# Gate and val of 256 tokens: half-block products by the seven-product scheme in place of full ones, in a dealt order, and last stores on two queues

**Chip, cores, metric.** One core of one Trainium2 chip. The metric is the device time of one execution in microseconds (us), the median over runs of one kernel on one chip.

## The reference

An attention block between 8 batches of 512 tokens and 32 state rows each (8 heads of 64) gives 8 x (512 + 32) rows of 512 values. A feed-forward block with RMS norm follows on all of them. The change concerns the feed-forward block of the 8 x 32 = 256 state rows:

```python
def _moe_ref(x, w_gate, w_val, w_out, rms_g):      # x: rows of 512, d_ff = 1536
    rms = np.sqrt(np.mean(x * x, axis=-1, keepdims=True) + 1e-06)
    xn = x / rms * rms_g
    g = xn @ w_gate
    silu = g * (1.0 / (1.0 + np.exp(-g)))
    val = xn @ w_val
    return (silu * val @ w_out).astype(np.float32)
```

## The kernel before

All is float32. The tokens of the batches come first. Gate and val of all batches but the first, and the output projections of these batches and of the states, are already done in seven products of half blocks instead of eight (the Strassen-Winograd scheme: a 2 x 2 block product costs seven half-block products, and some sums of blocks before and after). The states' 256 rows come last. Their gate and val were still full products: twelve hidden blocks m, for gate (k = 0) and val (k = 1) four contraction blocks i each, 256 columns at a time.

```python
    def hidden(m, n, lhs, rhs, banks):              # [... cut: set-up]
        def products():
            for k, to in enumerate((gp, vp)):
                to.append(banks[k].tile([P, S], F32, name=...))
                for i, r in enumerate(rhs):
                    TE.matmul(out=to[0][:, 0:n], lhsT=lhs(i, k), rhs=r,
                              start=(i == 0), stop=(i == len(rhs) - 1))
                yield
        def silu():  ...                            # ScalarE: Silu of gate, PSUM to SBUF
        def gated(): ...                            # VectorE: times val; for the upper blocks two more sums
# [... cut: the batches]
    for m in range(NM):                             # the states' stretch: NM = 12
        n = B * (NM // 2) + m // 2
        for part in hidden(m, NT, lambda i, k: w_sb[n][:, i, m % 2, k, :],
                           [xsT[:, i, :] for i in range(NI)], ((fx, fx), (fy, fz))[m % 2]):
            for _ in part:
                pass
        if m % 2:
            fetch(n + W_BUFS)                       # W_BUFS = 3: the weights of the pair after next but one
    p, c, k = project_seven(NT, store_states)       # products, copies, sums of the output projection
    for step in (p, c, p, c, k, p, k, p, c, k, p, k, p, k, p, c):
        next(step)
```

The pools of PSUM, the memory that TensorE writes its products to: a bank is one buffer of such a pool; `fx` has two banks, `fy` and `fz` one each. The weights of a pair of hidden blocks are one megabyte, in one of three buffers; a buffer is refilled when its pair has been multiplied for the last time.

## Time and profile before

| | before |
|---|---|
| time, median (runs) | 806.35 us (806.14 to 807.25, 3 runs) |
| span in the profile | 804.3 us |
| TensorE busy | 779.2 us, 97% |
| granted TensorE clock, mean | 0.989 |
| states' gate and val on TensorE | 192 records, 41.4 us |
| last copy's end to the end of the span | 3.84 us |

How to read it: the chain that ended last is the work followed back from the last instruction, at each step to what released it; the granted clock is the share of its full clock at which TensorE was let run. An engine that is busy 97% of the span and that makes up 94% of this chain is the bound; work of the others counts only where TensorE waits for it. TensorE makes two records of each float32 matmul (192 for the 96 here). The length printed for a record (379 ns) is longer than its share of the time, since records overlap; their spacing, from start to start (0.2158 us here), is what adds up. The lines are in the prediction.

### The profile page before, as it was taken

Reading aid. Unit: us, or ns where it says so; the run is one execution under the profiler, and the core shown is the slowest. Engines: PE = TensorE matmul, PEld = TensorE weight load, DVE = VectorE, ACT = ScalarE, POOL = GpSimd, SP = SyncE. Lnnn points to the kernel's source line nnn. Section 1 sums busy time; section 2 is a strip of 40 time slices with the busy share of each in tenths; the row PEclk is TensorE's granted clock in tenths of the full one; section 3 lists DMA queues with packets and bytes.
Section 4 is the critical chain, followed back from the end, with each engine's and each line's share of the span. In section 5 each row is a group of like instructions: output and inputs, shape, how many; then the busy total and the mean of one; then the engine's idle time right before and its main releaser. Section 6 shows DMA issues by size and latency. Waiting matters only on the chain.

```text
span 804.3 us, 11772 instructions
## 1 busy us (share of the span) xinstructions
PE 779.2 (97%) x4678; PEld 592.5 (74%) x4678; DVE 493.3 (61%) x746; ACT 341.1 (42%) x560; POOL 178.4 (22%) x215
## 2 busy tenths in 40 slices
PE   4599999999999999999999999999999999999997
PEld 2243444788778887888778877888788877888886
DVE  4999996588347842786368834784278626841121
ACT  4888864553245323543255324532354325401110
POOL 0000003530154005500443025400550044200000
PEclk9699999999999999999999999999999999999999
DMA  9788745600172007300460017200630035001401
GB/s 294 229 287 298 262 160 185 259 31 13 36 269 105 1 24 248 152 1 18 150 241 17 14 44 261 106 1 20 233 115 2 13 145 208 2 14 38 147 12 27
DMA packets 61591, 94.09 MB, mean 117 GB/s; under 512 B 38752, under 2 KB 46432, under 8 KB 54624
## 3 DMA queue, kind: packets, MB, share of 16 engines
q1 hardware_dynamic: 59456, 92.81, 33.4%
q8 instruction: 37, 0.61, 0.3%
q10 hardware_dynamic: 2080, 0.52, 0.3%
q14 instruction: 18, 0.15, 0.1%
HBM read 78.12 MB, written 15.20 MB: 116 GB/s over the span
## 4 chain that ended last, share of the span: by engine, by line
PE 94%; DVE 4%; issue 0%; ACT 0%; DMA 0%; SPq 0%; DVEq 0%
PE f L677 35%; PE f L527 32%; PE f L486 5%; PE f L617 5%; PE pv L486 4%; PE at L444 3%; PE pv L444 3%; PE at L273 2%; PE at L282 1%; PE at L327 1%; PE at L341 1%; PE at L388 1%; DVE ex L223 1%; PE at L376 1%; DVE raw L219 1%; PE at L252 1%
## 5 line engine op out<-in xcount | busy, mean ns | idle before, releaser
L677 PE MATMUL f<-wo,hb 128*128 128x256 f32 x540 | 124.1, 382 | 0.6 <-ACT ot L710 0.5
L527 PE MATMUL f<-aT_s,v 128*128 128x256 f32 x504 | 119.6, 381 | 0.0
L677 PEld LDWEIGHTS f<-wo,hb 128*128 128x128 f32 x540 | 101.4, 190 | 20.5 <-ACT ot L710 7.3
L527 PEld LDWEIGHTS f<-aT_s,v 128*128 128x128 f32 x504 | 93.7, 190 | 17.3 <-issue 5.2
L589 DVE TENSOR_TENSOR g<-g,f 128x512 f32<-128x512 f32 x84 | 57.6, 687 | 78.2 <-PE f L527 74.9
L245 POOL TENSOR_TENSOR ri<-ss,mhalf 128x4 f32<-128x4 f32 x8 | 9.1, 1141 | 364.4 <-DVE ss L345 364.4
L527 PE MATMUL f<-aT_t,vs 128*128 128x256 f32 x336 | 87.1, 382 | 0.0
L677 PE MATMUL f<-wt,hs 128*128 128x256 f32 x360 | 80.3, 379 | 0.0
L677 PEld LDWEIGHTS f<-wt,hs 128*128 128x128 f32 x360 | 68.4, 190 | 9.3
L527 PEld LDWEIGHTS f<-aT_t,vs 128*128 128x128 f32 x336 | 62.6, 190 | 15.4 <-issue 6.2
L710 ACT COPY ot<-f 128x256 f32<-128x256 f32 x60 | 21.4, 371 | 121.6 <-PE f L677 121.6
L580 ACT ACTIVATE hb<-g 128x1024 f32<-128x1024 f32 x42 | 44.4, 1057 | 55.0 <-DVE g L589 55.0
L591 DVE SCALAR_TENSOR_TENSOR hb<-hb,g 128x1024 f32<-128x1024 f32 x42 | 55.4, 1320 | 8.0 <-ACT hb L580 8.0
L473 POOL TENSOR_TENSOR vs<-v,vs 128x256 f32<-128x256 f32 x42 | 58.3, 1388 | 0.0
L470 POOL TENSOR_TENSOR vs<-v 128x256 f32<-128x256 f32 x42 | 30.6, 728 | 118.5 <-ACT v L455 118.5
L578 ACT COPY g<-f 128x512 f32<-128x512 f32 x42 | 24.6, 586 | 67.4 <-PE f L527 67.4
L486 PE MATMUL pv<-aT_s,v 128*128 128x512 f32 x96 | 45.2, 611 | 1.1 <-DVE aT_s L351 1.1
L617 PE MATMUL f<-wo,hb 128*128 128x512 f32 x96 | 44.7, 600 | 0.0
L527 PE MATMUL f<-aT_t,v 128*128 128x256 f32 x168 | 43.9, 383 | 0.0
L527 PE MATMUL f<-aT_s,vs 128*128 128x256 f32 x168 | 43.1, 379 | 0.0
L677 PE MATMUL f<-wt,hb 128*128 128x256 f32 x180 | 42.5, 386 | 0.0
L486 PE MATMUL f<-xsT,w_m 128*128 128x256 f32 x192 | 42.1, 379 | 0.0
(116 smaller groups left out, 1213.7 us busy)
## 6 DMA issues: line engine op xcount, KB each, us to landing
w_m<-w_d SPq DMA_DIRECT2D x48, 1024.0 KB, 6.6
x_b<-in_x_dram SPq DMA_DIRECT2D x30, 256.0 KB, 4.0
out_dram<-ot SPq DMA_DIRECT2D x56, 128.0 KB, 1.8
raw<-in_moe_w_val_dram SPq DMA_DIRECT2D x6, 1024.0 KB, 5.2
raw<-in_moe_w_out_dram SPq DMA_DIRECT2D x6, 1024.0 KB, 7.1
w_d<-w_m SPq DMA_DIRECT2D x6, 1024.0 KB, 4.9
raw<-in_moe_w_gate_dram SPq DMA_DIRECT2D x5, 1024.0 KB, 5.7
raw<-in_moe_w_gate_dram SPq DMA_DIRECT2D x2, 512.0 KB, 4.9
```

Source lines behind the costliest of these rows:

```text
L444: TE.matmul(out=pv[e][Ns * j:Ns * j + Ns, :], lhsT=stT_g[b][D * e:D * e + D, j, :], rhs=w[D * e:D * e + D, j].rearrange("p m k f -> p (m k ...
L470: GE.tensor_tensor(out=vs[:, 0], in0=a21, in1=a22, op=ALU.add)
L473: GE.tensor_tensor(out=vs[:, 2], in0=a12, in1=vs[:, 1], op=ALU.subtract)
L486: TE.matmul(out=to[0][:, 0:n], lhsT=lhs(i, k), rhs=r, start=(i == 0), stop=(i == len(rhs) - 1))
L527: TE.matmul(out=ps[:, i, :], lhsT=lhs[:, i, :], rhs=rhs, start=(start and i == 0), stop=True, skip_group_check=True)
L578: SE.copy(g[:, :, 1, :], q["x"])
L580: SE.activation(out=hb[:, 2 * mp:2 * mp + 2, :], func=ACTF.Tanh, scale=0.5, in_=g.rearrange("p m c t -> p m (c t)"))
L589: VE.tensor_tensor(out=to, in0=to, in1=q[ps], op=ALU.add)
L591: VE.scalar_tensor_tensor(out=h, in0=h, scalar=1.0, op0=ALU.add, op1=ALU.mult, in1=g.rearrange("p m c t -> p m (c t)"))
L617: TE.matmul(out=banks[r], lhsT=hb[:, m, P * r:P * r + P], rhs=wo[:, m, :], start=(m == 0), stop=(m == NM - 1))
L677: TE.matmul(out=banks[name][:, r, :], lhsT=lhs(k)[:, P * r:P * r + P], rhs=rhs(k), start=(start and r == 0 and k == 0), stop=(k == HM - 1) ...
L710: SE.copy(to, banks[name][:, r, :])
```

## The change

The intent is an eighth less work on TensorE in the states' gate and val. The function that did seven products for the batches is made general and used here too: seven products per pair of hidden blocks, each of 2 output blocks x 2 contraction blocks of 128 columns. For this VectorE must form sums of the weights (four per pair, 128x512 each) and of the tokens. Products (h), copies and Silu on ScalarE (t), sums after the products (u) and weight sums (y) are dealt to the engines by hand in one string; p, c, k are the projection. Apart from that the y-bank product of the states' projection is cut in two, and the last stores alternate between two queues.

```diff
+STATES = (
+    "hhtyythyhyyhthuhuyttuyuhhyhttuhhyhuhuhttuythyuhythuhyyhuuuhhthtythuuhtuyhhuhhtuh"
+    "yutyutuhthhhyhuuhuytuuththuhhuthuuuutuhuuppkcuppccppkkkpkpc"
+)
         # [... cut]
+    def sums_of_w(mps):
+        for mp in mps:
+            a11, a12, a21, a22 = blocks_of_w(mp)
+            ...
+            VE.tensor_tensor(out=s12[:, 0], in0=a21, in1=a22, op=ALU.add)
+            yield
+            VE.tensor_tensor(out=s12[:, 1], in0=s12[:, 0], in1=a11, op=ALU.subtract)
+            yield
+            VE.tensor_tensor(out=s4, in0=a12, in1=s12[:, 1], op=ALU.subtract)
+            yield
+            VE.tensor_tensor(out=a21, in0=a11, in1=a21, op=ALU.subtract)
+            yield
         # [... cut: views of blocks, sums of the tokens]
         def product(ps, lhs, rhs, start):
             for i in range(2):
-                TE.matmul(out=ps[:, i, :], lhsT=lhs[:, i, :], rhs=rhs, start=(start and i == 0),
-                          stop=True, skip_group_check=True)
+                for k, (l, r) in enumerate(zip(lhs, rhs)):
+                    TE.matmul(out=ps[:, i, 0:half], lhsT=l[:, i, :], rhs=r, ...)
         # [... cut: in project_seven, for the states only]
-            yield from product("y", A(0, 1), B(1, 0))
+            parts = (range(HM),) if R > 1 else (range(HM // 2), range(HM // 2, HM))
+            yield from product("y", A(0, 1), B(1, 0), parts[0])
             yield from product("x", S_, TS(1))
+            for ks in parts[1:]:
+                yield from product("y", A(0, 1), B(1, 0), ks)
         # [... cut: store_states]
-            nc.sync.dma_start(out=out[r0:r0 + Ns, c0:c0 + n], in_=...)
+            queue = (nc.sync, *more)[j % (1 + len(more))]
+            queue.dma_start(out=out[r0:r0 + Ns, c0:c0 + n], in_=...)
         # [... cut: the loop over m goes]
+    h, t, u = hidden_seven(NT, (state_weights, state_sums), state_tokens, True,
+                           lambda mp: fetch(n + mp + W_BUFS))
+    p, c, k = project_seven(NT, store_states, nc.scalar)
+    streams = {"h": h, "t": t, "u": u, "p": p, "c": c, "k": k, "y": sums_of_w(range(1, NM // 2))}
+    with tc.manual_schedule(**by_hand):
+        for stream in STATES:
+            next(streams[stream])
```

Each pair has the products x, z, x, z, y, x into the banks of these names, then the next pair's first x and z, then its own last x ("last product").

## The prediction

> **What bounds the kernel now.** I read the page's busy times first: TensorE is busy nearly the whole span and no other engine comes near it. Then the chain that ended last, from 742 us on, which is where the changed stretch lies:

> ```profile
> PE 779.2 (97%) x4678; PEld 592.5 (74%) x4678; DVE 493.3 (61%) x746; ACT 341.1 (42%) x560; POOL 178.4 (22%) x215
> ...
> 742.33 38.85 PE f L486 x180
> 781.18 10.37 PE f L677 x48
> 791.55 0.02 issue
> 791.58 0.38 ACT ot L710
> 791.96 0.04 issue
> 792.00 8.05 PE f L677 x36
> 800.05 0.02 issue
> 800.08 0.37 ACT ot L710
> ```

> L486 is gate and val of the states' 256 tokens, L677 their output projection, L710 a copy out of PSUM. The path is TensorE alone, except for 0.46 us at 791.55 (a copy stands between two products into the same bank) and the tail after 800.05. L486 runs at 38.85 / 180 = 0.2158 us per record. It has 96 matmuls of 256 columns, two records each, so 192 x 0.2158 = 41.4 us in all; 12 of the records are used earlier as filling in the last batch's projection (three gaps of 4 records, 0.86 us each). The other engines idle here: between 742.4 and 781.2 VectorE is busy 7.6 us and ScalarE 4.6 us (busy times by stretch, summed). So removing TensorE work there should shorten the kernel one for one, unless a new wait appears.

> The group rows of the old stretch, and two places elsewhere that show what a short record costs:

> ```profile
> L486 PE MATMUL f<-xsT,w_m 128*128 128x256 f32 x192 | 42.1, 379 | 0.0
> L486 PEld LDWEIGHTS f<-xsT,w_m 128*128 128x128 f32 x192 | 36.5, 190 | 5.0
> ...
> 692.67 1.84 PE L412 MATMUL at<-ones,sqT 128*128 128x1 f32 x16
> 694.38 0.89 PE L527 MATMUL f<-aT_s,v 128*128 128x256 f32 x3
> ...
> 603.13 0.60 PE L273 MATMUL at<-ident,x_b 128*128 128x128 f32 x4
> 603.57 1.03 PE L527 MATMUL f<-aT_t,v 128*128 128x256 f32 x4
> ```

> From start to start, sixteen records of one column with a full weight load each take (694.38 - 692.67) / 16 = 0.107 us: there the weight load is the bound. Four transposes of 128 columns take 0.44 / 4 = 0.11 us. The 190 ns of a load's own row is its length, not its spacing.

> [...] No float32 matmul of 128 columns that isn't a transpose is in this trace; whether two such nearly equal halves overlap fully is my largest uncertainty. [...]

> **The change part by part.**

> *Products.* Per pair of hidden blocks seven products of half blocks: 7 x 2 output blocks x 2 contraction blocks = 28 matmuls of 128 columns, 56 records; six pairs make 336 records. At 0.110 us: 37.0 us against 41.4, a gain of 4.4 us. One product (8 records) is a step of 0.88 us, there are 42 steps.

> *Added VectorE and ScalarE work.* Per pair VectorE has three sums from PSUM and two products (0.42 us each, as 128x256 sums from PSUM show), for the upper three pairs two more, and four weight sums of 128x512 (0.69 us, from such rows). In the stretch itself that is about 15 x 0.69 + 36 x 0.42 = 25.5 us of 37: no bound by quantity. ScalarE's three copies and one Silu per pair are under 2 us of each pair's 6.2.

> *Weights' arrival.* This is where I expect most of the gain to go. Only three weight buffers exist, so pairs 3, 4, 5 are fetched when pairs 0, 1, 2 have had their last product. These fetches are in the trace of before, where nothing waits for them:

> ```profile
> L143 SPq DMA_DIRECT2D w_m<-w_d x3: 320/327/327, 746.7 to 760.5; - x3
> ...
> DMA to landing us min/median/max: 4.6/4.7/4.8
> ```

> Before, such a megabyte is first read two pairs later by TensorE. Now VectorE must first make sums of it, and the dealt order of VectorE has the first sum of pair 3's weights directly behind pair 0's last product and ahead of pair 1's sum out of the z bank. Sequence after pair 0's last product ends: landing 4.75 us later, weight sum 0.69, z sum 0.42, so the z bank is free after 5.9 us. TensorE has five steps (4.4 us) until it needs this bank, the only one of its kind: it waits 1.5 us. For pair 4's weights two weight sums stand ahead of the z sum: 4.75 + 1.38 + 0.42 = 6.6 us against 4.4, a wait of 2.2 us. Pair 5's first sum stands a whole pair later in the order (after 6.2 us, landed by then): no wait. Together 3.7 us back.

> *Last batch's tail.* The filling is now 6, 2 and 6 records (0.66, 0.22, 0.66 us). A copy needs about 0.48 us, so the middle gap stays open by 0.26. The states' norm and sums on VectorE (four of 0.42 and four more of 0.42) come ahead of the last pair's gating and push the sum that the next product's fifth matmul needs from 707.2 to 710.2, where TensorE gets to it at about 710.1: 0.1 us.

> *Projection.* Same 84 records, 18.1 us. The y product is cut in two and placed between the products that share a bank: the 0.46 us at 791.55 goes.

> *Last stores.* The rows:

> ```profile
> L746 SPq DMA_DIRECT2D out_dram<-ot x16: 314/419/423, 789.5 to 801.8; - x16
> ...
> DMA to landing us min/median/max: 1.5/1.6/1.6
> ...
> 800.47 1.71 SPq L746 DMA_DIRECT2D out_dram<-ot  x4
> ```

> Four issues, 0.43 us apart, the last at 801.76; landed 1.6 us later, and 0.9 us to the end of the span. Two on each of two queues start the last at about 800.9: 0.85 us less.

> *Sum:* -4.4 +3.7 +0.26 +0.1 -0.46 -0.85 = -1.7 us, so 806.35 - 1.7 = 804.7 us, 0.2% faster.

> **Rivals.**

> *A: everything stays hidden.* The dealt order was made so that nothing waits; if the weights landed in some 3 us, or their sums ran ahead of need, the 3.7 us would not be lost: 801.0 us. For it: the rows of before have no idle TensorE anywhere in the batches, whose products were dealt in the same way. Against it: 4.6 us to landing, three times of three, and the position in VectorE's order, which can be read from the built program.

> *B: short records don't overlap with their weight loads.* [...] For it: the two durations are almost equal, there is no slack for either. Against it: 0.107 us per full load in the trace is already the bare load, and transposes of 128 columns ran at 0.11.

> *C: VectorE becomes the bound.* 25.5 of 37 us plus waits in order; if each pair loses another microsecond to order, 6 us: again 810. Against it: I walked the order pair by pair and found only the two places above.

> **Range and chances.** The gain at stake is at most 4.4 + 0.46 + 0.85 = 5.7 us, or 0.7%, so 2% (16 us) faster is out of reach, and 16 us slower would need records of over 0.15 us. Low end: rival A nearly whole, 801.5. High end: half way into B or C, 808.5. Chances: faster by over 2% 0.01, within 2% 0.97, slower by over 2% 0.02.

> **What would show it.** Right: the 336 records of 128 columns spaced 0.110 us where TensorE doesn't wait; VectorE's first sum of pair 3's and of pair 4's weights waiting for the weights' DMA, and TensorE idle behind them about 1.5 and 2.2 us; no idle for pair 5; no copy on the chain within the states' projection; the end 0.85 us nearer to the last copy. Wrong: spacing of 0.12 us or more (B), no TensorE idle behind the DMA (A), or VectorE busy without gaps through the stretch (C). A shift of more than 1 us in the batches before 700 us would mean that the change touches something that I left out.

The forecast's sum came to -1.7 us, and what carries its 0.110 us per record is the transposes' 0.11 us. The "two such nearly equal halves" are a record's weight load (0.107 us in the trace) and its matmul, by an estimate half of the 0.2158 us of 256 columns, so 0.108 us. That a waiting sum holds up what VectorE has behind it was taken for granted in the forecast of the waits. Rival C itself is 804.7 + 6 = 810.7 us, and half way into it 807.7; no sum is shown for the 808.5 of the range.

## The result

| | before | after |
|---|---|---|
| time, median | 806.25 us (4 runs) | 808.62 us (808.06 to 809.18, 4 runs) |
| ratio, 95% interval | | 1.0027 (1.0009 to 1.0044) |
| span in the profile | 804.3 us | 806.2 us |
| granted clock, mean | 0.989 | 0.979 |

Ratios are computed as the mean time of one kernel's runs over that of the other's of the same rounds, so they are not quite the ratio of the medians. The change costs 0.3%; it is slower, not faster, though well within 2%. The median lies 0.1 us above the predicted range.

The lower mean clock is not by itself the loss. Of the 0.010 between the two profiles 0.002 belongs to the stretch examined below (3.4 us at half clock in 806); nearly all the rest lies in the first 50 us (0.83 before, 0.69 after), after which the same product near 706 us starts only 0.16 us later.

The chain that ended last of the changed kernel, from the start of the stretch (start us, us, what), answers to the chain of before. L596 is the states' gate and val, L750 their output projection, L787 a copy out of PSUM, L553 a weight sum, L658 a sum that reads a PSUM bank:

```profile
741.86 6.49 PE f L596 x58
...
748.37 4.77 DMA w_m<-w_d
...
753.16 0.04 DVE v L553
...
753.77 0.43 DVE g L658
...
754.25 2.06 PE f L596 x16
...
756.33 4.84 DMA w_m<-w_d
...
763.00 19.77 PE f L596 x160
...
782.79 0.43 DVE c L658
...
783.27 1.16 PE f L596 x8
784.42 18.23 PE f L750 x84
...
802.68 0.37 ACT ot L787
```

Twice the chain leaves TensorE (L596) for the arrival of weights, comes to a weight sum on VectorE (L553), to the z sum behind it (L658: the sum that reads, and so frees, the z bank), and back. Once, at the end, it goes through a sum of the c tile. Before, the same stretch was a single line of TensorE. The stretch with its projection is 802.66 - 741.86 = 60.80 us long, before 800.05 - 742.33 = 57.72. TensorE's busy time is no help in finding this: it is 97% in both kernels.

The first wait in order of time on VectorE, with what ended the idle time in brackets:

```profile
748.38 0.42 DVE L667 TENSOR_TENSOR hb<-hb,f 128x256 f32<-128x256 f32 x1 [0.68 <-PE f L596]
753.16 0.69 DVE L553 TENSOR_TENSOR v<-w_m 128x512 f32<-128x512 f32 x1 [4.37 <-DMA w_m<-w_d]
753.77 0.75 DVE L658 TENSOR_TENSOR g<-g,f 128x256 f32<-128x256 f32 x2
```

VectorE does nothing for 4.37 us in front of a weight sum that TensorE needs only at the first z product of pair 3, while the sum behind it (L658, the z bank's) is what TensorE waits for. And TensorE about the second wait, where the end of the record before it is modelled some 0.17 us late:

```profile
763.00 1.90 PE L596 MATMUL f<-x_t,v 128*128 128x128 f32 x8 [2.23 <-DVE g L658]
764.68 1.91 PE L596 MATMUL f<-x_t,w_m 128*128 128x128 f32 x8
766.39 1.18 PE L596 MATMUL f<-x_t,v 128*128 128x128 f32 x8
767.40 1.06 PE L596 MATMUL f<-xsT,vs 128*128 128x128 f32 x8
```

Eight records take 0.893 us undisturbed (24 records from 743.71 to 746.39 us: 0.1116 us each). From 763.00 to 766.39 us each eight takes 1.7 us. The view by stretches says why; its columns are the stretch and its length, busy time and number of instructions of TensorE, its weight loads, VectorE, ScalarE and GpSimd, the granted TensorE clock, and the DMA engines' share and GB/s:

```profile
754.30:760.60 6.30, 6.30 (x56) 6.27 (x56) 3.12 (x7) 1.63 (x4) 0.00 (x0) 1.00 0.46 166
760.70:762.90 2.20, 0.06 (x1) 0.00 (x0) 1.67 (x4) 0.00 (x0) 0.00 (x0) 1.00 0.00 0
763.00:766.40 3.40, 3.40 (x17) 3.40 (x18) 1.54 (x4) 1.26 (x3) 0.00 (x0) 0.53 0.02 5
```

Right after the idle 2.4 us TensorE ran at half its clock for 3.4 us. This was in no step of the prediction.

**Where the 2 us went.** By the records' spacing, in the two profiles:

| term | predicted | measured |
|---|---|---|
| 336 records at 0.110 / 0.1116 us, against 41.4 us | -4.4 | -3.9 |
| first wait (752.64 to 754.25) | +1.5 | +1.6 |
| second wait (760.60 to 763.00) | +2.2 | +2.4 |
| half clock behind it (32 records in 5.30 us, not 3.57) | none | +1.7 |
| last pair: 782.59 to 783.27 | none | +0.7 |
| gap in the last batch's projection (0.4), slower records around the short ones (0.2) | +0.26 | +0.6 |
| VectorE's norm and sums ahead of a product | +0.1 | 0 |
| restarts behind the first and the last wait | none | +0.2 |
| states' projection (18.87 to 18.24 us) | -0.46 | -0.6 |
| end: 3.84 to 3.20 us | -0.85 | -0.6 |
| start of the kernel (706.01 against 705.85 us at the same product) | none | +0.16 |
| two transposes (713.62 us in before) now run ahead of that product | none | -0.2 |
| sum | -1.7 | +2.0 |

A restart is the slower first eight records behind a wait (0.99 us instead of 0.893). The spans differ by 1.96 us.

### The profile page after: what moved, and what is told of

The parts are those of the page before. It is cut to its first block, busy times and chain, and to the rows that moved or that the text cites. A ratio compares the mean times of both kernels' runs of the same rounds, so it can differ in the third digit from the quotient of the medians. Undisturbed runs are those within 1.5% of the kernel's fastest.

```text
span 806.2 us, 12107 instructions
## 1 busy us (share of the span) xinstructions
PE 778.8 (97%) x4822; PEld 596.3 (74%) x4822; DVE 514.4 (64%) x786; ACT 346.8 (43%) x572; POOL 177.9 (22%) x215
## 4 chain that ended last, share of the span: by engine, by line
PE 92%; DVE 4%; DMA 2%; ACT 1%; issue 1%; SPq 0%; DVEq 0%
PE f L596 36%; PE f L750 35%; PE f L690 5%; PE pv L492 4%; PE at L450 3%; PE pv L450 3%; PE at L278 2%; DMA w_m<-w_d 1%; PE at L332 1%; PE at L287 1%; PE at L346 1%; PE at L393 1%; PE at L381 1%; DVE ex L228 1%; DVE raw L224 1%
## 5 line engine op out<-in xcount | busy, mean ns | idle before, releaser
L750 PE MATMUL f<-wo,hb 128*128 128x256 f32 x540 | 124.2, 382 | 0.4 <-ACT ot L787 0.2
L596 PE MATMUL f<-aT_s,v 128*128 128x256 f32 x504 | 119.5, 380 | 0.0
L658 DVE TENSOR_TENSOR g<-g,f 128x512 f32<-128x512 f32 (+1 forms) x96 | 62.6, 654 | 88.5 <-PE f L596 85.2
L750 PEld LDWEIGHTS f<-wo,hb 128*128 128x128 f32 x540 | 101.4, 190 | 20.1 <-ACT ot L787 6.9
L596 PEld LDWEIGHTS f<-aT_s,v 128*128 128x128 f32 x504 | 93.8, 190 | 17.4 <-issue 5.2
L596 PE MATMUL f<-aT_t,vs 128*128 128x256 f32 x336 | 87.2, 382 | 0.0
L750 PE MATMUL f<-wt,hs 128*128 128x256 f32 x360 | 80.4, 379 | 0.0
L649 ACT ACTIVATE hb<-g 128x1024 f32<-128x1024 f32 (+1 forms) x48 | 48.2, 1004 | 69.9 <-DVE g L658 69.9
L750 PEld LDWEIGHTS f<-wt,hs 128*128 128x128 f32 x360 | 68.3, 190 | 9.5 <-issue 0.2
L787 ACT COPY ot<-f 128x256 f32<-128x256 f32 x60 | 21.5, 372 | 122.5 <-PE f L750 122.5
L596 PEld LDWEIGHTS f<-aT_t,vs 128*128 128x128 f32 x336 | 62.6, 190 | 15.1 <-issue 5.9
L647 ACT COPY g<-f 128x512 f32<-128x512 f32 (+1 forms) x48 | 26.9, 561 | 77.6 <-PE f L596 77.6
L596 PE MATMUL f<-aT_t,v 128*128 128x256 f32 x168 | 43.9, 383 | 0.0
L596 PE MATMUL f<-aT_s,vs 128*128 128x256 f32 x168 | 43.1, 379 | 0.0
L750 PE MATMUL f<-wt,hb 128*128 128x256 f32 x180 | 42.6, 386 | 0.0
L750 PE MATMUL f<-wo,hs 128*128 128x256 f32 x180 | 41.6, 382 | 0.0
```

The costliest lines, as they stand in the source:

```text
L596: TE.matmul(out=ps[:, i, 0:half], lhsT=l[:, i, :], rhs=r, start=(start and i == 0 and k == 0), stop=(k == len(lhs) - 1), skip_group_check= ...
L647: SE.copy(gates(q)[1], q["x"][:, :, 0:half])
L649: SE.activation(out=hb[:, 2 * mp:2 * mp + 2, 0:n].rearrange("p m (c t) -> p m c t", c=2), in_=q["g"][:, :, :, 0:half], func=ACTF.Silu if s ...
L658: VE.tensor_tensor(out=to, in0=to, in1=q[ps][:, :, 0:half], op=ALU.add)
L750: TE.matmul(out=banks[name][:, r, :], lhsT=lhs(k)[:, P * r:P * r + P], rhs=rhs(k), start=(start and r == 0 and k == 0), stop=(k == HM - 1) ...
L787: SE.copy(to, banks[name][:, r, :])
```

## The experiments

My theory after the result: the sparing of records is real; it is eaten by the order on VectorE (weight sums that wait for their weights in front of sums that TensorE needs) and by the clock that the idle time costs. The rivals: the short records, or the sparse use of the array, bring the half clock by themselves; the weights' arrival is a bound in any order; the slow records have another reason than the clock.

A first idea, a fourth weight buffer so that the weights come earlier, does not fit: the pool of seven output tiles then lacks room (7 KB per partition asked, 3.3 KB left). It did not build.

The first four ran on one chip (kernel before on it: 806.42 us, 9 runs).

### sums_later: both weight sums moved

Only VectorE's order changes: pair 3's four weight sums (y) go behind pair 1's gated halves, pair 4's behind pair 2's. TensorE's and ScalarE's orders are the same as in the changed kernel.

```diff
-    "hhtyythyhyyhthuhuyttuyuhhyhttuhhyhuhuhttuythyuhythuhyyhuuuhhthtythuuhtuyhhuhhtuh"
+    "hhtyythyhyyhthuhuyttuyuhhyhttuhhhuhuhttuthuyyhthuyyhhuuuhhthtthuyyuyyhtuhhuhhtuh"
```

> The weight sums of pairs 3 and 4 are moved on VectorE behind the work that TensorE waits for; TensorE's order and all work stay as in the changed kernel. Theory (order on VectorE plus the clock that the idle time costs): both waits of TensorE behind the z sum (1.6 and 2.4 us from the modelled end of the last record before them) go, and so does the stretch at half clock behind the second (1.7 us): 5.7 us less, about 802.9 us where the changed kernel gives 808.6. Rival 1 (the half clock belongs to the short records or their sparse use of the array, not to the idle time): the half-clock stretch stays, 804.6 us. Rival 2 (the arrival of the weights is a bound in any order, and the wait turns up at the next product that needs their sums): 807 to 808.6 us.

802.10 us (801.73 to 803.54, 5 runs), ratio to before 0.9950 (0.9937 to 0.9962). The chain:

```profile
741.75 35.08 PE f L596 x314
776.82 0.02 issue
776.85 0.43 DVE c L658
777.28 0.04 issue
777.32 1.16 PE f L596 x8
778.48 18.23 PE f L750 x84
```

Both waits are gone, 314 records run on end (the short wait before the last eight is still there), and the clock record has no half-clock stretch in this part of the span (granted clock 1.00 from 741.75 to 776.60 us). The change's own order was the loss, not the scheme: rivals 1 and 2 of this run fall. It is also 0.5% faster than before.

### first_later and second_later: one of the two moved

```diff
 first_later
-    "hhtyythyhyyhthuhuyttuyuhhyhttuhhyhuhuhttuythyuhythuhyyhuuuhhthtythuuhtuyhhuhhtuh"
+    "hhtyythyhyyhthuhuyttuyuhhyhttuhhhuhuhttuthuyyhthuyyhyyhuuuhhthtythuuhtuyhhuhhtuh"
 second_later
-    "hhtyythyhyyhthuhuyttuyuhhyhttuhhyhuhuhttuythyuhythuhyyhuuuhhthtythuuhtuyhhuhhtuh"
+    "hhtyythyhyyhthuhuyttuyuhhyhttuhhyhuhuhttuythyuhythuhhuuuhhthtthuyyuyyhtuhhuhhtuh"
```

> Only pair 3's weight sums are moved. Theory: the first wait (1.6 us) goes, the second (2.4 us) stays, and the half-clock stretch behind it stays or not [...]: 807.0 us with it, 805.3 without. Rival (the second wait is a consequence of the first): both go, 803 us.

> Only pair 4's weight sums are moved. Theory: the first wait (1.6 us) stays with no half clock behind it, the second and the half-clock stretch go: 4.1 us less than the changed kernel, 804.5 us. If 1.6 us of idle time can trip the throttle too, up to 1.7 us more.

first_later: 806.08 us (804.76 to 806.33, 5 runs), ratio 0.9992 (0.9980 to 1.0005). Its profile shows no first wait, the second one of 2.4 us, and half clock from 762.09 to 765.50 us:

```profile
741.85 12.74 PE f L596 x114
...
754.61 4.85 DMA w_m<-w_d
...
761.28 19.77 PE f L596 x160
```

So the second wait is no consequence of the first. The median is 0.9 us below the 807.0 that was expected with half clock, and the five times spread over 1.6 us, which is followed up below.

second_later: 804.69 us (803.96 to 805.11, 5 runs), ratio 0.9977 (0.9965 to 0.9990), as expected: the first wait of 1.6 us is there, soon behind it (from 756.02 us) the records are spaced 0.1116 us, and no half clock follows:

```profile
755.03 24.40 PE f L596 x216
```

### filled: the second idle time filled with idle work

```diff
+                if silu and mp == 3:
+                    idle = aps.tile([P, NC, P], F32, name="at")
+                    for j in range(10):
+                        TE.matmul(out=idle[:, 0, :], lhsT=a11[0][:, 0, :], rhs=b11[0],
+                                  start=True, stop=True)
                 q["z"] = fz.tile([P, 2, HS], F32, name="f")
```

> The changed kernel with ten extra matmuls of 128 columns (20 records, 2.2 us), into an unused bank and never read, just where TensorE idles the second time. They remove no wait: the product behind them still waits for VectorE's z sum. Theory (idle time alone drops the clock): the granted clock stays full behind the wait, 1.7 us less, 806.9 us. Rival (the slow records after the wait are slow for another reason, such as VectorE's sums or the weights' arrival): the records after the wait stay at 0.21 us, 808.6 us.

806.37 us (805.72 to 806.84, 5 runs), ratio 0.9999 (0.9985 to 1.0012). The chain behind the first wait, L611 being the idle matmuls:

```profile
754.68 6.52 PE f L596 x56
761.20 2.23 PE at L611 x20
763.44 18.11 PE f L596 x160
```

The 160 records that took 19.77 us in the changed kernel take 18.11 here, although VectorE's sums and the weights' arrival are where they were. Doing useless work there is worth 1.7 us in the profile: the granted clock is 1.00 from 763.40 to 766.80 us, where the changed kernel had 0.53 behind its wait. The slow records come from the idle time before them: the rival of this run falls.

### first_later_b, _c, _d: three more looks at first_later

> The kernel with only pair 3's sums moved, looked at again, because its five times spread over 1.6 us, as much as the half-clock stretch costs. Theory: the wait of 2.4 us is there in each look, the half-clock stretch of 3.4 us [...]; with it some 806 us, without it some 804.5 us. Rival: the stretch is always there and the spread has another source (the clock in the first 50 us).

> A second look of the same kind: a wait of 2.4 us, and with the half-clock stretch some 806 us, without it some 804.5 us (theory); the stretch in every look (rival).

> A third look of the same kind: a wait of 2.4 us, and with the half-clock stretch some 806 us, without it some 804.5 us (theory); the stretch in every look (rival).

The theory is that the stretch comes in some looks and not in others.

The three looks gave 804.50, 806.21 and 805.46 us. In none was there a half-clock stretch behind the wait, though the wait was there each time (2.25 us in the profile's row of the first):

```profile
761.08 1.16 PE L596 MATMUL f<-x_t,v 128*128 128x128 f32 x8 [2.25 <-DVE g L658]
762.07 1.06 PE L596 MATMUL f<-x_t,w_m 128*128 128x128 f32 x8
```

and in its chain the records that took 19.77 us above take

```profile
761.08 18.15 PE f L596 x160
```

So the rival (always there) falls. But 806.21 us without the half clock says that part of the spread does have another source, before the stretch: in that look the states' stretch starts 1.8 us later than in the first (743.44 against 741.63 us). Half clock near the start of the kernel, which ends at 41.7 to 45.0 us in the profiles that record it, may be that source: in the eight profiles, of the kernels that share all work before the stretch (all but before and ends_only), where it ends at 42.6 us or later, the stretch starts at 741.6 us with the earliest end and at 743.4 us with the latest, with one small inversion between. No run was made for it.

Counted from the start of the states' stretch to the end of the span, this spread drops out: 64.4 and 64.3 us in the two profiles of the changed kernel, 62.7 in first_later with the half clock and 61.0 to 61.1 in its three looks without it, 60.3 in second_later, 58.6 in sums_later and 57.8 in best (below). By this measure too the half clock costs 1.6 to 1.7 us, within one and the same kernel.

| look | idle from, to | grid edge near it | idle time before the edge, behind it | half clock behind the wait |
|---|---|---|---|---|
| after, second wait | 760.60, 763.00 | 763.22 | 2.40, 0 | yes |
| after_again (below), second wait | 760.30, 762.65 | 762.83 | 2.35, 0 | yes |
| first_later | 758.88, 761.28 | 762.09 | 2.40, 0 | yes |
| first_later_b | 758.66, 761.08 | 759.45 | 0.79, 1.62 | no |
| first_later_c | 760.47, 762.75 | 761.76 | 1.29, 0.99 | no |
| first_later_d | 759.74, 762.05 | 760.71 | 0.97, 1.34 | no |
| after, first wait | 752.64, 754.25 | 752.98 | 0.34, 1.26 | no |
| after_again, first wait | 752.35, 753.95 | 752.59 | 0.24, 1.36 | no |
| second_later | 753.41, 755.03 | 754.22 | 0.81, 0.81 | no |

Of the waits, the three with 2.35 us or more of their idle time between two edges were followed by half clock (for 3.41 us from 763.22 us in after and from 762.09 us in first_later; in after_again the 160 records behind the wait again took 19.77 us), and the six with at most 1.62 us between two edges were not. That it is this division which decides is the reading of nine cases; no run moved a wait against the grid to test it.

### best, products_only, ends_only, and the changed kernel again

These four ran on one chip (kernel before on it: 806.48 us, 9 runs). best is sums_later with one letter moved: the first product of the projection (p) goes between the last pair's third and last x product (the last h).

```diff
-    "yutyutuhthhhyhuuhuytuuththuhhuthuuuutuhuuppkcuppccppkkkpkpc"
+    "yutyutuhthhhyhuuhuytuuththuhhuthuuuutuphuupkcuppccppkkkpkpc"
```

products_only is sums_later with `parts = (range(HM),)`, the projection's letters `pcpckupkpckpkpkpc` at the end, and without the second queue. ends_only is the kernel before with the two other parts of the change:

```diff
-    p, c, k = project_seven(NT, store_states)
-    for step in (p, c, p, c, k, p, k, p, c, k, p, k, p, k, p, c):
-        next(step)
+    p, c, k = project_seven(NT, store_states, nc.scalar)
+    with tc.manual_schedule(**by_hand):
+        for step in (p, p, k, c, p, p, c, c, p, p, k, k, k, p, k, p, c):
+            next(step)
```

> The kernel with both weight sums moved, and besides the first product of the states' projection set between the last pair's third x product and its fourth, between which TensorE waited 0.68 us for VectorE's sum (776.64 to 777.32 us by the records' spacing). Theory: that wait goes and no other comes, as the second projection product's first eight records (1.7 us) cover the 0.9 us that VectorE needs after the last product: 801.4 us where sums_later gave 802.1. Rival (the wait moves to the second projection product): 802.1 us.

> The kernel with both weight sums moved, without the two other parts of the change: the y product of the states' projection is whole again in the order of before, and the last stores go out on one queue. Theory: 0.6 us more in the projection (18.87 us of before against 18.24) and 0.7 us more at the end (3.85 us of before from the last copy's end to the span's against 3.15): 803.4 us. If the products gave nothing and the ends all: 806 us.

> The kernel before with only the split y product in the new order and the last stores on two queues. Theory: 0.6 + 0.7 us less than before, 805.1 us. Rival (the last stores' landing does not depend on the issuing queue): 805.8 us.

> The changed kernel once more, on the same chip as the three others, as the reference for them: 808.6 us, with the half clock after the second wait in the profile again.

| kernel | median (range, 5 runs) | ratio to before, 95% interval |
|---|---|---|
| best | 801.52 us (801.24 to 802.63) | 0.9939 (0.9926 to 0.9951) |
| products_only | 803.72 us (803.10 to 804.70) | 0.9965 (0.9953 to 0.9978) |
| ends_only | 804.78 us (804.68 to 805.61) | 0.9979 (0.9967 to 0.9992) |
| after_again | 808.07 us (807.52 to 808.48) | 1.0018 (1.0004 to 1.0032) |

The products alone, in an order that waits only before the last of them, are worth 806.48 - 803.72 = 2.8 us, the two ends 1.7 us, and together 802.10 in sums_later: the parts add up (2.8 + 1.7 = 4.5 against 806.42 - 802.10 = 4.3). In the profile of ends_only the projection takes 18.23 us and 3.2 us lie between the last copy's end and the span's, as in the changed kernel. best in the place of the last wait:

```profile
743.02 35.06 PE f L596 x314
778.08 2.59 PE f L750 x12
780.67 0.89 PE f L596 x8
781.56 15.64 PE f L750 x72
```

No wait is left in the stretch. Its median is 0.6 us below that of sums_later, as expected, though the two ran on different chips and their intervals overlap; from the start of the stretch to the end of the span its profile is 0.8 us shorter. best beats the kernel before by 0.6% and the changed kernel by 0.8% on the same chip (801.52 against 808.07 us).

## Why the prediction was right or wrong

**Right: what the products cost.** The estimate of 0.110 us per record measured 0.1116. Rival B, that the load and the matmul would not overlap, falls: a record with its full weight load was spaced 0.1116 us, where records of one column with such a load were spaced 0.107.

**Right: the two waits, their place and their cause.** 1.5 and 2.2 us were predicted, 1.6 and 2.4 measured, with the weights landing in 4.77 and 4.84 us on the chain. Rival A, that the dealt order hides everything, falls; first_later and second_later show that each wait hangs on its own sums. For pair 5 TensorE didn't wait, as predicted; VectorE did for 0.65 us.

**Wrong: the sum, in its sign.** "*Sum:* -4.4 +3.7 +0.26 +0.1 -0.46 -0.85 = -1.7 us" counted each wait at its length. The term that is missing is the clock: the second wait cost 1.7 us more, in records behind it at half speed. filled shows it. This term alone brings the sum to 0. I had the granted clock at 1.00 in all of the old stretch and didn't ask what a new gap does to it. That the time came so close to the top of the range is luck: the top was set for rivals B and C, and neither happened.

**Wrong: "found only the two places above".** The walk ended before the last pair. There the third x product, the sum on VectorE that reads its bank and the last x product into the same bank follow each other with nothing in between; in all other pairs two products of the next pair stand there. It cost 0.7 us, and best removes it.

**Sizes.** The last batch's gap measured 0.4, not 0.26 us, and the records around the short ones cost 0.2 more. The projection gained 0.6 and not 0.46 us (in before, the 36 records behind the wait also took 8.05 us where their spacing of 0.2158 us gives 7.77; part of that went too). The end gained 0.6 and not 0.85 us: both queues' last issues start near 803.5 us, 0.4 us behind the first, as predicted, yet 2.7 us then pass to the end of the span where I had carried over 2.5 from before. These and the other rows of the table, above all the clock and the last pair, make up the 3.7 us between -1.7 and the measured 2.0. One slip changed nothing: against rival A the text gives the landing as 4.6 us three times of three, where its own row has 4.6 to 4.8.

**What stays open.** How much idle time it takes for the clock to drop. The ends of two profiles lie closest: behind TensorE's last record, by the spacing, 2.26 us are idle up to the next edge of the grid in first_later (800.79 to 803.05 us), and half clock follows; in first_later_c 2.10 us are idle (800.63 to 802.72 us), and none follows. That is one case on each side, and no run was made between them.

And why all nine timed runs of the changed kernel lie at 807.5 us or more, so probably all with the half-clock stretch (two were looked at in a profile), while three of four looks at first_later had none. The kept traces suggest an answer. In nine of the eleven profiles of kernels that share all work before the stretch the states' stretch starts 698.4 to 699.1 us behind the grid edge at which the half clock near the start ends (in first_later_d, which records none there, the edge at which its record begins); in first_later and sums_later it starts 700.0 us behind. Placed on these grids, the changed kernel's second wait, 18.7 us into the stretch, lies whole between two edges in the nine and is split by one in the two; that of first_later, 17.0 us into it, is split in the nine and whole in the two. If the division decides, half clock would mostly follow in the changed kernel and seldom in first_later; this is worked out from the traces, and no run moved the start to test it.

## What to carry to other kernels

VectorE ran its work here in the dealt order: it stood idle for 4.37 us before a weight sum while the z sum dealt behind it was what TensorE waited for. Work that waits for a transfer must then stand behind everything that the bounding engine needs, and this can be read from the built order and one landing time (4.77 us here) before anything runs. A wait of the bounding engine is not always worth its length: 2.4 us of idle TensorE cost 4.1 us in the changed kernel, where half clock followed (+1.7), and about 2.4 in the looks at first_later where none did (61.0 to 61.1 us from the start of the stretch against 58.6 in sums_later). When a walk through a dealt order finds where it waits, walk also its first and last round, where the neighbours that filled the gaps are missing.
